# Gated mix of dilated attention and a 2-D Fourier filter: ScalarE's table read, one fp32 block, the gate sums and the issue order changed

## The chip, the cores and the metric

The kernel runs on one NeuronCore of a Trainium2 chip. A core has five engines with instruction streams of their own: TensorE (PE, the matmuls; its weight loads are listed as PEld), VectorE (DVE), ScalarE (ACT), GpSimd (POOL) and SyncE (SP, which here only starts transfers). Every engine takes its instructions strictly in the order in which the program issues them; engines wait for one another through semaphores. ACT, SP and POOL also start DMA transfers. The metric is the device time of one execution in microseconds (us).

## The reference, cut to what matters

Inputs are `x` (2048 x 640), the weights `wqkv` (640 x 1920) and `wo` (640 x 640), a filter `w_r`, `w_i` (2048 x 321) and the gate vector `gate_w` (640); all fp32.

```python
g = sigmoid((x * gate_w).sum(-1, keepdims=True))
# a: attention, 32 heads of 20, each row looks at rows s, s-2, ..., s-14
qkv = x @ wqkv
logits = einsum("bhsd,bhswd->bhsw", q, k gathered at s - 2*w) * 20**-0.5   # w = 0..7, masked below 0
a = (softmax(logits) weighted sum of v) @ wo
# b: filter in the frequency domain over both axes
b = irfft2(rfft2(x) * (w_r + 1j * w_i))
out = g * a + (1 - g) * b
```

## The kernel before

**Tiling.** Row `s = 16 p + j` of `x` lies on partition `p`, index `j`, so a step of two rows is a step of two in `j`. The even `j` ("par 0", tile `xe`) and the odd `j` ("par 1", tile `xo`) never meet in the attention. The columns of `wqkv` are cut into four groups `hg` of 8 heads. A unit `u = 4*par + hg` is one of the eight matmul stages `qkv0` to `qkv7`; it feeds two attention halves `a` and `b`.

**Precision.** A matmul in plain fp32 stands in the trace as two instructions and is slow, so nearly every fp32 product is split: `hi` is the operand rounded to fp32r (a cast on ACT), `lo` the remainder (a subtraction on DVE or POOL), and three fast products `hi*hi + hi*lo + lo*hi` take the place of one. `w` (weights) and `xe`, `xo` are such pairs. Only the blocks listed in `WHOLE` (line 1142) are multiplied in plain fp32, straight from the raw tiles `st`: before, these are row blocks 0 and 1 of the first 128 inner columns, the very first products of the kernel (`qkv_first`, line 679).

**Stages, in the order in which they were recorded.** `warm` (line 611): a DVE memset and six dummy matmuls. `load_first` (654): the five slices of the first column group, `in_w0`, started by ACT, and the five slices of the even rows, `in_xE`, started by SP (slice 0 in two pieces of 3 and 4 row blocks), then the casts on ACT and the subtractions on DVE. Then, for all eight units: products into one of seven PSUM banks, a copy to `ev` on ACT (two such tiles take turns, `store`, 722) and a DMA to DRAM (`qkvd`). The next weights go through `raw` (SP), a cast on ACT and a subtraction (`load_w`, 633). `attend` (746) reads `kt`, `q`, `vt` back: DVE and POOL form products `pr` and `pv` and DVE sums them to `L` and `o`; `o` goes to DRAM (`od`). On DVE and POOL `fold` (827) prepares the Fourier input, `cols` (855) and sixteen `freq` groups (877) transform it. Within a `freq` group PE forms `v` and `u`, ACT copies `vs`, DVE forms `ab`, PE forms `x` and `z`, ACT scales them into `X`, a pair of DMAs exchanges halves (`P<-X`), POOL and DVE multiply by the filter `wp` to `s`, and PE forms `g`, which ACT copies back into `zg`. `spatial` (1003) is the way back along the columns; `project_even` and `project_odd` (1085, 1101) multiply the attention output by `wo`. Odd projections need the attention of par 1, of which units 5 and then 4 come last.

**Gates.** `gates` (738) runs once, when all 16 row sums `z` are there: one exponential on ACT and four small DVE operations on 128 x 16 elements.

**What sets the order of the work.** The operations are first only recorded (`Plan.record`, 230): 3,656 of them, 1,977 on PE, 522 on DVE, 656 on ACT, 309 on POOL and 192 on SP. Then a list scheduler in the kernel file (`cost`, `order`, `forward`, `backward`, lines 249 to 437) gives each operation a made-up duration and latency (for instance 3.2 us for a transfer to land, 2 us added from POOL to ACT), computes due times and issues the operations in the order of the starts that it computes; a list of 32 random seeds (`FOUND`) perturbs it. That order is what the engines execute.

Of the kernel before, what the change touches and what calls it, by code (L numbers as in the profile page):

```python
# [11 lines left out]
ALU = mybir.AluOpType  # L12
# [16 lines left out]
PAGE = 512  # L29
# [120 lines left out]
class Op:  # L150
    __slots__ = ("i", "eng", "name", "call", "busy", "lat", "size", "preds", "succs", "chain", "tail", "start", "end", "early", "group", "of", "two")
# [12 lines left out]
class Plan:  # L164
# [4 lines left out]

    def __init__(self, nc):  # L170
        self.ops, self.places, self.past = [], {}, set()
        self.chain = self.group = ""
# [10 lines left out]
    def region(self, ap):  # L183
        off, pat = ap.offset, list(ap.ap)
        p0, p1 = 0, 1
        if ap.tensor.tag[:4] != "dram":
            p0 = off // pat[0][0]
            off, p1, pat = off - p0 * pat[0][0], p0 + pat[0][1], pat[1:]
        if ap.tensor.tag[:4] == "bank":
            off, pat = 0, [(1, 512)]  # L190
        idx = np.array([off])
        for st, n in pat:
            idx = (idx[:, None] + st * np.arange(n)).reshape(-1)
        return p0, p1, np.unique(idx)

    def touch(self, op, ap, write):

        if not hasattr(ap.tensor, "tag"):
            return
        tag, name = ap.tensor.tag, ap.tensor.name  # L200
        place = self.places.setdefault(tag, [name, {}, set()])
        if place[0] != name:
            assert name not in self.past, f"{name} used again after {place[0]}"
            self.past.add(place[0])
            self.places[tag] = place = [name, {}, {acc[0] for page in place[1].values() for acc in page}]
        pages, before = place[1:]
        if write:
            op.preds |= before
        p0, p1, idx = self.region(ap)
        size = PAGE if p1 > 1 else 1 << 30  # L210
        for pg in np.unique(idx // size):
            mine = idx[idx // size == pg]
            lo, hi, dense = mine[0], mine[-1], len(mine) == mine[-1] - mine[0] + 1
            kept = []
            for acc in pages.get(pg, ()):
                o, w, q0, q1, alo, ahi, adense, aidx = acc
                hit = o is not op and q0 < p1 and p0 < q1 and alo <= hi and lo <= ahi
                if hit and not (dense and adense):
                    hit = len(np.intersect1d(mine, aidx, assume_unique=True)) > 0
                if hit and (w or write):  # L220
                    op.preds.add(o)
                covered = write and hit and p0 <= q0 and q1 <= p1
                if covered:
                    covered = lo <= alo and ahi <= hi if dense else len(np.setdiff1d(aidx, mine, assume_unique=True)) == 0
                if not covered:
                    kept.append(acc)
            kept.append((op, write, p0, p1, lo, hi, dense, mine))
            pages[pg] = kept

    def record(self, eng, name, fn, a, k):  # L230
        op = Op()
        op.i, op.eng, op.name, op.chain, op.group = len(self.ops), eng, name, self.chain, self.group
        op.preds, op.succs, op.size, op.early, op.two = set(), [], 0, False, False
# [5 lines left out]
        aps = [v for v in list(a) + list(k.values()) if hasattr(v, "tensor") and hasattr(v, "ap")]  # L239
        out = k["out"] if "out" in k else a[0]  # L240
        ins = [v for v in aps if v is not out]
        for v in ins:
            self.touch(op, v, False)
        self.touch(op, out, True)
        op.of = out.tensor.name
        self.cost(op, out, ins, k)
        self.ops.append(op)

    def cost(self, op, out, ins, k):
        n = max(int(np.prod(v.shape[1:])) for v in [out] + ins[:1])  # L250
        if op.name == "dma_start":
            op.busy, op.lat = {"SP": 0.45, "ACT": 0.45, "POOL": 1.0}[op.eng], LAND
            op.size = int(np.prod(out.shape)) * 4
            op.early = not hasattr(ins[0].tensor, "tag")
        elif op.eng == "PE":
            n = int(np.prod(out.shape[1:]))
            if op.name == "transpose":
                op.busy = 0.109
            elif ins[-1].dtype == F32R:
                op.busy = n / 2400 + 0.018  # L260
            else:
                op.busy = 4 * n / 2400 + 0.006
            op.lat = 0.25
        elif op.eng == "DVE":
            op.busy, op.lat = 0.075 + n / 960, 0.12
            two = sum(v.tensor.tag[:4] not in ("bank", "qban") for v in ins) == 2
            if op.name == "scalar_tensor_tensor":
                op.busy += 0.06
            elif op.name == "reciprocal":
                op.busy += n * 0.007  # L270
            elif two:
                op.two = True
        elif op.eng == "ACT":
            strided = any(len(v.ap) > 2 and v.ap[-1][0] > 1 for v in [out] + ins)
            op.busy, op.lat = 0.12 + n * (1.75e-3 if strided else 0.78e-3), 0.15
            if len(ins) > 1:
                op.busy += 0.1
        else:
            spread = any(v.ap[-1][0] == 0 for v in ins)
            op.busy, op.lat = 0.09 + n * (2e-3 if spread else 2.25e-3), 0.14  # L280
        if op.eng in ("DVE", "ACT", "POOL") and not op.size:
            op.busy *= PACE

    def order(self):
        ops = self.ops
        for op in ops:
            op.lat += LATE.get(op.chain, 0.0) * (not op.size or op.chain in ("swap", "f"))
        for op in ops:
            for p in op.preds:
                p.succs.append(op)  # L290
        last = {}
        for op in reversed(ops):
            op.tail = max([s.tail + self.lag(op, s) for s in op.succs], default=0.0)
            if op.size:
                op.tail += op.size / RATE
            key = (op.eng, op.chain)
            if key in last and (op.eng == "PE" or op.chain and op.eng != "ACT"):
                op.tail = max(op.tail, last[key].tail)
            op.tail += op.busy
            last[key] = op  # L300
        span = max(op.tail for op in ops)
        for op in ops:
            op.early = max(0.0, span - op.tail - AHEAD) if op.early else 0.0
            op.tail += BIAS.get(op.chain, 0.0)
        best = self.turns(TURNS)

        kinds = [op.of for op in ops], [op.of.rstrip("0123456789_") for op in ops], [op.eng + op.of.rstrip("0123456789_") for op in ops]
        kinds = [[k[:4] if i else k for k in kind] for i, kind in enumerate(kinds)]
        self.kinds = []
        for kind in kinds:  # L310
            at = {k: i for i, k in enumerate(dict.fromkeys(kind))}
            self.kinds.append((len(at), np.array([at[k] for k in kind])))
        for seed in FOUND:
            for op, t in zip(ops, (best[1] + self.move(seed)).tolist()):
                op.tail = t
            best = self.turns(2)
        self.end = best[0]
        order = []
        for op, op.start, op.end in best[2]:
            order.append(op)  # L320
        return order

    def turns(self, n):

        runs = []
        for i in range(n + 1):
            tails = np.array([op.tail for op in self.ops])
            done = self.forward()
            end = max(op.end + op.lat for op in done)
            runs.append((end, tails, [(op, op.start, op.end) for op in done]))  # L330
# [880 lines left out]
```

## Time and profile before

| what | us |
|---|---|
| three runs | 460.13, 461.62, 462.81 |
| median | 461.62 |
| span of the profiled execution, first to last instruction | 459.8 |
| busy: PE, DVE, POOL, ACT | 442.6, 414.2, 364.3, 212.4 |

The profile is of one execution, on the one core. Its span leaves out what lies around the instructions; the median of the runs is 1.8 us longer. The busy time of PE counts a matmul that waits in the pipeline as busy. Times in the timeline count from the start of the span. `[idle before <-releaser]` behind a row says how long that engine was idle before it and whose end released it.

### The profile page before, as it was taken

How to read it: one execution, taken by the hardware profiler on the slowest of the kernel's cores; microseconds unless marked ns; L12 is line 12 of the kernel's file. 1: busy time of each engine (PE TensorE's matmuls, PEld its weight loads, DVE VectorE, ACT ScalarE, POOL GpSimd, SP SyncE). 2: the span in 40 equal slices, each digit the busy share in tenths (PEclk: the TensorE clock that was granted, in tenths of full speed). 3: DMA queues.
4: the chain of work that ended last, by engine and by line, in shares of the span. 5: the costliest groups of instructions: out<-in, count | busy, mean ns of one | idle time of the engine just before them, and what ended most of it. 6: DMA issues, size and time to landing. Idle time of an engine off the chain costs nothing.

```text
span 459.8 us, 7244 instructions
## 1 busy us (share of the span) xinstructions
PE 442.6 (96%) x2440; PEld 391.3 (85%) x2440; DVE 414.2 (90%) x522; ACT 212.4 (46%) x558; POOL 364.3 (79%) x316
## 2 busy tenths in 40 slices
PE   9999979999999999999997889999988999999996
PEld 6888868888889889899886778989977899988996
DVE  3898988999999998999999999899999998799574
ACT  4623235533326545246447666666554554342110
POOL 1158796699999988997997997886899997888820
PEclk9999989999999999999999999999999999999999
DMA  8998989768878979579979788889983331365842
GB/s 308 399 358 260 390 284 375 273 218 300 229 220 231 329 221 324 144 240 333 295 221 291 254 264 238 261 247 296 251 271 123 83 97 44 118 195 146 280 137 86
DMA packets 73956, 110.75 MB, mean 241 GB/s; under 512 B 21296, under 2 KB 50992, under 8 KB 73920
## 3 DMA queue, kind: packets, MB, share of 16 engines
q1 hardware_dynamic: 40192, 69.32, 46.6%
q10 hardware_dynamic: 32816, 36.97, 25.9%
q0 software_dynamic: 912, 4.00, 2.2%
q8 instruction: 19, 0.31, 0.3%
q14 instruction: 17, 0.14, 0.1%
HBM read 72.51 MB, written 32.84 MB: 229 GB/s over the span
## 4 chain that ended last, share of the span: by engine, by line
PE 78%; DMA 10%; POOL 4%; DVE 2%; ACT 2%; issue 1%; ACTq 1%; POOLq 0%; DVEq 0%
PE qkv L615 41%; PE woa L615 6%; PE wob L615 6%; DMA P<-X 5%; PE z L615 5%; PE oa L615 4%; PE ob L615 4%; DMA qkvd<-ev 3%; POOL P L615 3%; PE g L615 2%; DMA q0a<-qkvd 2%; PE hb L615 2%; PE ha L615 2%; PE v L615 2%; PE u L615 1%; PE oTp L615 1%
## 5 line engine op out<-in xcount | busy, mean ns | idle before, releaser
L615 PE MATMUL qkv<-w,xo 128*128 128x480 f32 (+1 forms) x480 | 110.8, 386 | 0.0
L615 PE MATMUL qkv<-w,xe 128*128 128x480 f32 (+1 forms) x474 | 106.2, 386 | 2.8 <-ACT w L615 2.8
L615 PEld LDWEIGHTS qkv<-w,xe 128*128 128x128 f32 x474 | 90.5, 191 | 18.7 <-ACT w L615 3.2
L615 PEld LDWEIGHTS qkv<-w,xo 128*128 128x128 f32 x480 | 89.8, 189 | 13.8 <-ACT zg L615 0.2
L615 ACT COPY ev<-qkv 128x480 f32<-128x480 f32 x64 | 35.1, 559 | 74.1 <-PE qkv L615 60.7
L615 PE MATMUL woa<-wo,oT 128*128 128x320 f32 x240 | 47.2, 318 | 0.6 <-DVE oT L615 0.3
L615 PE MATMUL wob<-wo,oT 128*128 128x320 f32 x240 | 46.9, 316 | 0.2 <-ACT ya L615 0.2
L615 POOL TENSOR_TENSOR P<-P,wp 128x963 f32<-128x963 f32 (+1 forms) x16 | 35.5, 2216 | 12.1 <-DMA P<-X 5.9
L615 PEld LDWEIGHTS woa<-wo,oT 128*128 128x128 f32 x240 | 37.7, 188 | 1.6 <-DVE oT L615 0.9
L615 PEld LDWEIGHTS wob<-wo,oT 128*128 128x128 f32 x240 | 37.8, 188 | 0.6 <-ACT ya L615 0.4
L615 POOL TENSOR_TENSOR fx<-fx 128x160 f32<-128x160 f32 (+1 forms) x16 | 12.2, 780 | 27.1 <-DVE fx L615 21.9
L615 POOL TENSOR_TENSOR w<-raw,w 128x480 fp32r<-128x480 f32 (+1 forms) x20 | 25.5, 1296 | 4.1 <-ACT w L615 4.1
L615 ACT CAST oT<-oTp 128x384 fp32r<-128x384 f32 (+1 forms) x32 | 13.4, 428 | 32.4 <-PE oTp L615 18.8
L615 PEld LDWEIGHTS g<-mm,s 128*128 128x128 f32 x150 | 21.2, 190 | 8.0 <-ACT zg L615 5.1
L615 PE MATMUL g<-mm,s 128*128 128x128 f32 x150 | 23.7, 280 | 4.1 <-ACT zg L615 3.2
L615 DVE TENSOR_TENSOR oT<-oTp,oT 128x384 fp32r<-128x384 f32 (+1 forms) x32 | 15.2, 484 | 10.0 <-ACT oT L615 9.9
L615 PE MATMUL oa<-gt,zg 128*128 128x161 f32 (+1 forms) x96 | 24.0, 344 | 0.0
L615 ACT CAST w<-raw 128x480 fp32r<-128x480 f32 (+1 forms) x30 | 17.2, 593 | 13.3 <-PE qkv L615 5.4
L615 PE MATMUL v<-bt,zc 128*128 128x240 f32 (+2 forms) x96 | 21.1, 325 | 1.9 <-ACT vs L615 1.8
L615 PE MATMUL ob<-gt,zg 128*128 128x161 f32 (+1 forms) x96 | 22.1, 344 | 0.0
L615 PE MATMUL u<-bt,zc 128*128 128x240 f32 (+2 forms) x96 | 20.3, 324 | 1.7 <-DVE ab L615 1.7
L615 PEld LDWEIGHTS u<-bt,zc 128*128 128x128 f32 x96 | 16.2, 189 | 4.1 <-DVE ab L615 1.2
(304 smaller groups left out, 1118.9 us busy)
## 6 DMA issues: line engine op xcount, KB each, us to landing
qkvd<-ev ACTq DMA_DIRECT2D x32, 480.0 KB, 4.8
wp<-in_ws SPq DMA_DIRECT2D x16, 642.0 KB, 5.6
raw<-in_wqkv SPq DMA_DIRECT2D x25, 240.0 KB, 6.8
fx<-in_x SPq DMA_DIRECT2D x8, 641.0 KB, 8.2
ot<-od SPq DMA_DIRECT2D x16, 320.0 KB, 3.4
P<-X ACTq DMA_DIRECT2D x30, 160.5 KB, 4.1
fd<-fx POOLq DMA_DIRECT2D x6, 640.0 KB, 7.5
f<-fd SPq DMA_DIRECT2D x6, 640.0 KB, 6.3
```

The source lines that it names most:

```text
L615: p.dve.memset(w, 0.0)
```

## The change

1. **Table read.** `warm` gets one more operation on ACT: a copy of one column of the zeroed tile. In the trace before, ACT's first computing instruction is preceded by an ACT_TABLE_LOAD.
2. **First transfers.** Slice 1 of `in_w0` is started by SP in place of ACT (`W0_SP`).
3. **One fp32 block for two.** `WHOLE` keeps (0, 0); block (1, 0) becomes three split products.
4. **Gate sums.** Three of the four DVE operations of `gates` (`1 + e`, `g - 1`, `1 - g`) become ACT operations; the reciprocal stays on DVE.
5. **Order.** The scheduler is gone. The operations are still recorded in the same sequence, and are issued in an order stored as a compressed string.

```diff
     def order(self):
-        ops = self.ops
...
-        return order
+        low, high = np.frombuffer(lzma.decompress(base64.b85decode("".join(ORDER.split()))), np.uint8).reshape(2, -1)
+        left, at = list(self.ops), low + 256 * high.astype(int)
+        assert len(at) == len(left)
+        return [left.pop(i) for i in at]
...
+ORDER = """
+T>t<81poj4|NsC0{{R326$?I)!2u1*Nf}?AmSE|uhAe8`yGLM)dM(g$Y~TpLBZIqd7Xw}I)19wZeN}MiGV`E!kd>$bRcBSWDq9b1%rA=d_}B$A_%Oua6Qw8m;-l*ba;C<oxwBJ%2Z0mn
...
         p.dve.memset(w, 0.0)
+        p.act.copy(self.one("tab", 1, tag="sign"), w[:, 0:1])
...
-            p.act.dma_start(self.wraw[0, t], self.ins["w0"][t])
+            (p.sp if t in W0_SP else p.act).dma_start(self.wraw[0, t], self.ins["w0"][t])
...
         p.act.activation(out=self.g, in_=self.z, func=AF.Exp, scale=-1.0)
-        p.dve.tensor_scalar_add(self.g, self.g, 1.0)
+        p.act.activation(out=self.g, in_=self.g, func=AF.Copy, bias=1.0)
         p.dve.reciprocal(self.g, self.g)
-        p.dve.tensor_scalar_sub(self.nng, self.g, 1.0)
-        p.dve.tensor_scalar(out=self.ng, in0=self.g, scalar1=-1.0, scalar2=1.0, op0=ALU.mult, op1=ALU.add)
+        p.act.activation(out=self.nng, in_=self.g, func=AF.Copy, bias=-1.0)
+        p.act.activation(out=self.ng, in_=self.g, func=AF.Copy, scale=-1.0, bias=1.0)
...
-WHOLE = ((0, 0), (1, 0))
+WHOLE = ((0, 0),)
+W0_SP = (1,)
```

The string unpacks to 3,659 numbers, two bytes each: 3,656 operations, one copy and two matmuls more. Each number is the place, in the list of recorded operations not yet issued, of the next one. Read out against the recorded sequence, the first operations of two queues are, side by side:

| ACT before | ACT after | SP before | SP after |
|---|---|---|---|
| start w0 slice 0 | start w0 slice 0 | start xE slice 0, blocks 0-2 | start xE slice 0, blocks 3-6 |
| start w0 slice 1 | start w0 slice 2 | start xE slice 0, blocks 3-6 | start w0 slice 1 |
| start w0 slice 2 | start w0 slice 3 | start xE slice 1 | start xE slice 1 |
| start w0 slice 4 | copy tab | start xE slice 2 | start xE slice 0, blocks 0-2 |
| start w0 slice 3 | start w0 slice 4 | start xE slice 3 | start row block 14 (xT) |
| cast w0 slice 0 | cast xE slice 0, blocks 3-6 | start xE slice 4 | start xE slice 3 |
| cast xE slice 0, blocks 0-2 | cast w0 slice 0 | start fx0 | start xE slice 2 |

Behind the six dummy matmuls, PE's list before begins with the two fp32 blocks; after, with seventeen split products of row blocks 3 to 6, and the one fp32 block left is the 24th entry of PE's list.

Four places further on, as entries of each engine's own list counted from 0:

| place | before | after |
|---|---|---|
| ACT: cast of `w2_3` | 71 | 65 |
| ACT: first copy of `ev1_4` / of `ev1_6` | 59 / 70 | 69 / 74 |
| PE: first product that reads `w2_3` / `w2_4` | 258 / 272 | 268 / 293 |
| PE: first product that reads `w3_3` / `w3_4` | 371 / 374 | 326 / 329 |

(`w2_3` is slice 3 of the weights of unit 2.)

More of the change, by code (lines that the diff above doesn't have):

```diff
@@ L1 @@
+import base64
+import lzma
 import sys
-from heapq import heapify, heappop, heappush
 import numpy as np
@@ L150 @@
 class Op:
-    __slots__ = ("i", "eng", "name", "call", "busy", "lat", "size", "preds", "succs", "chain", "tail", "start", "end", "early", "group", "of", "two")
+    __slots__ = ("i", "eng", "name", "call")
 class Engine:
@@ L170, in __init__ @@
     def __init__(self, nc):
-        self.ops, self.places, self.past = [], {}, set()
-        self.chain = self.group = ""
+        self.ops = []
         self.code = {}
@@ L196, in touch @@
[L196 to L228, printed above, removed]
@@ L230, in record @@
     def record(self, eng, name, fn, a, k):
         op = Op()
-        op.i, op.eng, op.name, op.chain, op.group = len(self.ops), eng, name, self.chain, self.group
-        op.preds, op.succs, op.size, op.early, op.two = set(), [], 0, False, False
+        op.i, op.eng, op.name = len(self.ops), eng, name
         line = sys._getframe(2).f_lineno
@@ L238, in record @@
         op.call = (code, {"fn": fn, "a": a, "k": k})
[L239 to L246, printed above, removed]
-        self.ops.append(op)
[L249 to L282, printed above, removed]
@@ L284, in order @@
-    def order(self):
-        ops = self.ops
[L286 to L320, printed above, removed]
-        return order
@@ L323, in turns @@
[L323 to L330, printed above, removed]
-            if i < n:
-                self.backward(end)
-        return min(runs, key=lambda r: r[0])
-    def move(self, seed):
-        rng = np.random.default_rng(seed)
-        n, kind = self.kinds[rng.integers(3)]
-        shift = rng.choice([0.6, 2.0, 6.0, 15.0]) * rng.normal(size=n)
-        return (shift * (rng.random(n) < rng.choice([0.03, 0.1, 0.4, 1.0])))[kind]
@@ L465, in staged @@
+HnU*@@RtAPIC%5
+"""
 def staged(gens, n):
```

170 lines of the change are left out of this document (31 added, 139 removed).

## The prediction

> **What bounds the kernel now.** The busy times on the page come first, then the waits of PE over the whole span, then the table of stretches.
>
> ```profile
> PE 442.6 (96%) x2440; PEld 391.3 (85%) x2440; DVE 414.2 (90%) x522; ACT 212.4 (46%) x558; POOL 364.3 (79%) x316
> ```
> ```profile
> PE g L615 <- ACT zg L615: 3.2, 5, 1.3
> PE qkv L615 <- ACT w L615: 2.8, 1, 2.8
> PE v L615 <- ACT vs L615: 1.8, 1, 1.8
> PE u L615 <- DVE ab L615: 1.7, 2, 1.0
> ```
> ```profile
> 4.00:16.00 12.00, 12.00 (x44) 8.77 (x45) 7.54 (x14) 8.92 (x17) 0.00 (x0) 1.00 1.04 390
> ...
> 145.00:235.00 90.00, 90.00 (x477) 79.53 (x476) 86.42 (x76) 41.23 (x111) 81.79 (x63) 1.00 0.87 272
> 235.00:305.00 70.00, 63.79 (x375) 55.35 (x374) 65.05 (x101) 45.58 (x131) 58.97 (x50) 1.00 0.85 255
> 305.00:353.00 48.00, 45.05 (x288) 40.15 (x288) 45.59 (x68) 27.69 (x75) 41.34 (x31) 1.00 0.84 250
> 353.00:420.00 67.00, 66.43 (x415) 60.08 (x414) 60.36 (x86) 31.52 (x81) 58.68 (x49) 1.00 0.36 107
> 420.00:460.00 40.00, 36.18 (x255) 35.83 (x253) 26.16 (x58) 4.91 (x12) 17.43 (x22) 1.00 0.49 162
> ```
>
> In the table the columns are the stretch, its length, busy time (count) of PE, PEld, DVE, ACT and POOL, granted PE clock, DMA share and GB/s. PE is the bound, with 17.2 us of the 459.8 idle; DVE is close behind: 86.42 of 90 us in the longest stretch. So a gain has two forms: an idle place of PE that closes, or work that leaves DVE. The idle of PE sits in one hole near 62 us, and in the Fourier groups between 235 and 353 us (70.00 - 63.79 = 6.2 us and 48.00 - 45.05 = 2.9 us). Elsewhere PE is dense, so no stage can give more than these holes.
>
> **The hole at 62 us.** The timeline shows what ACT did while PE waited, and the stretches beside it show the clock.
>
> ```profile
> 63.85 0.56 ACT L615 COPY ev<-qkv 128x480 f32<-128x480 f32 x1 [2.24 <-DMA qkvd<-ev]
> 64.31 0.60 ACT L615 CAST w<-raw 128x480 fp32r<-128x480 f32 x1
> ...
> 64.95 10.37 PE L615 MATMUL qkv<-w,xe 128*128 128x480 f32 x39 [2.79 <-ACT w L615]
> ```
> ```profile
> 61.60:65.00 3.40, 0.61 (x4) 0.20 (x2) 3.37 (x3) 1.16 (x4) 3.40 (x4) 1.00 0.57 167
> 65.00:68.40 3.40, 3.40 (x9) 2.84 (x10) 2.17 (x2) 1.65 (x6) 3.40 (x5) 0.51 0.86 251
> 68.40:71.80 3.40, 3.40 (x17) 2.93 (x16) 3.33 (x4) 1.77 (x5) 1.98 (x2) 0.99 1.04 376
> ```
>
> ACT takes its list in order. The copy of `ev1_6` stood ahead of the cast of `w2_3` and waited for an `ev` transfer to free its tile; the cast needed no such thing, and PE needed the cast. The hole is 2.8 us, and behind it PE ran 3.4 us at a clock of 0.51: 9 matmuls where the next stretch has 17, so 8 x 0.2 = 1.6 us more (0.2 us is 3.40 / 17). **Price: 4.4 us.**
>
> By the stored order the cast of `w2_3` is ACT's 65th entry and the first copies of `ev1_4` and `ev1_6` are the 69th and 74th, so it no longer stands behind that wait. PE reads `w2_4` first at its entry 293, not 272: 21 matmuls later. What can come instead is late `w3`: PE now asks for `w3_4` 45 matmuls sooner, at entry 329. The pace for this is in the row below, 38.33 / 175 = 0.219 us.
>
> ```profile
> 23.83 38.33 PE L615 MATMUL qkv<-w,xe 128*128 128x482 f32 x175
> ...
> 74.75 0.59 ACT L615 CAST w<-raw 128x480 fp32r<-128x480 f32 x1
> ```
>
> Counting from the hole (entry 258, at 62.0 us), entry 329 falls at 62.0 + 71 x 0.219 = 77.5 us; the cast of `w3_4` ended at 75.3 us before, and its transfer and cast stand at nearly the same places of their lists. The margin is 2 us. I take 4.0 of the 4.4 us as gained; bounds: 4.4, and -4.4 if the same hole opens twice.
>
> **The gate sums.** Here are the four operations of DVE, the exponential of the same shape on ACT, and what stood around the longest.
>
> ```profile
> L615 ACT ACTIVATE g<-z x1: 223/223/223, 249.1 to 249.1; 128x16 f32<-128x16 f32 x1
> L615 DVE TENSOR_SCALAR g<-g x1: 823/823/823, 249.7 to 249.7; 128x16 f32<-128x16 f32 x1
> L615 DVE RECIPROCAL g<-g x1: 253/253/253, 250.5 to 250.5; 128x16 f32<-128x16 f32 x1
> L615 DVE TENSOR_SCALAR ng<-g x1: 4199/4199/4199, 270.5 to 270.5; 128x16 f32<-128x16 f32 x1
> L615 DVE TENSOR_SCALAR nng<-g x1: 518/518/518, 384.2 to 384.2; 128x16 f32<-128x16 f32 x1
> ```
> ```profile
> 269.85 2.66 POOL L615 TENSOR_TENSOR pv7b<-vt7b,L7b 128x640 f32<-128x640 f32 x2
> ...
> 270.45 4.20 DVE L615 TENSOR_SCALAR ng<-g 128x16 f32<-128x16 f32 x1
> ...
> 271.11 3.54 DVE L615 TENSOR_REDUCE L6b<-pr6b 128x64 f32<-128x1280 f32 x1
> ...
> 272.40 2.23 POOL L615 TENSOR_TENSOR P<-P,wp 128x963 f32<-128x963 f32 x1
> ...
> 274.73 0.94 PE L615 MATMUL u<-bt,zc 128*128 128x240 f32 x4 [0.97 <-DVE ab L615]
> ```
>
> Sixteen columns need 0.25 us on DVE, yet one of these took 4.20 us. It ended at 274.65, within 0.1 us of the end of the POOL work beside it (272.40 + 2.23 = 274.63), and the reduction issued behind it ended at 274.65 as well (271.11 + 3.54): DVE stood still until POOL was done, and PE then waited 0.97 us for `ab`. Gone from DVE are 0.82 + 4.20 + 0.52 = 5.5 us. ACT gets three operations of 0.22 us, and it is busy 45.58 of 70 us there; queued behind them are copies such as `vs`, which then come up to 0.7 us later. How much of the 5.5 us reaches the end isn't in a row: at least nothing, at most all of it less 0.7. DVE is over 90% busy up to 420 us, but PE would have to use the time. I take half, **2.5 us**; bounds 0 and 4.8.
>
> A rule stands against this edit: the Trainium skill, "ScalarE: Activation LUTs", section "Rules for kernel authors", sends plain additions and multiplications to VectorE and not ScalarE. Here 0.22 us on ACT stands against 0.52 to 4.20 us on DVE, so the trace disagrees.
>
> **The start.** These are the rows of the first microseconds.
>
> ```profile
> 0.74 3.51 ACTq L615 DMA_DIRECT2D st<-in_w  x5
> 0.75 5.48 SPq L615 DMA_DIRECT2D st<-in_xE  x6
> ...
> 1.06 2.93 PE L615 MATMUL warmed<-warm 128*128 128x128 f32 x12 [1.06 <-DVE warm L615]
> ...
> 3.94 3.41 PE L615 MATMUL qkv<-st,st 128*128 128x482 f32 x4
> 4.28 1.28 ACT L615 ACT_TABLE_LOAD   x1 [4.28 <-DMA st<-in_w]
> ...
> 5.58 0.59 ACT L615 CAST w<-st 128x482 fp32r<-128x482 f32 x1
> ...
> 6.07 0.51 ACT L615 CAST xe<-st 128x384 fp32r<-128x384 f32 x1
> ...
> 6.63 17.58 PE L615 MATMUL qkv<-w,xe 128*128 128x482 f32 x76
> ```
>
> The table read takes 1.28 us ahead of the first cast. After three transfers are issued (0.74 + 3 x 0.70 = 2.85 us; 0.70 is 3.51 / 5) the new copy lets it run until 4.1 us, and the copy itself ends by 4.3 us. The fourth issue stands behind the copy, so slice 4 may start 0.7 us later than before; it is cast last. On SP the moved transfer delays every later issue by 5.48 / 6 = 0.9 us, but the DMA share is 1.04 between 4 and 16 us, so the data, not the issues, set the landings. ACT can thus cast 1.3 us earlier. PE loses its fill, though: the two fp32 blocks ran from 3.94 to 6.63 us while ACT was still at it, and now PE's first product needs two casts, which end at about 4.3 + 0.6 + 0.6 = 5.5 us. Two blocks stand for six split products; between 5.5 and 6.63 us PE can do at most five at the pace of 17.58 / 76 = 0.23 us, and three at the half clock. So PE is 0.3 to 0.8 us behind. The block itself gives a little back: two of the four passes (half of 2.7 us, or half of that at full clock) go and 3 x 0.23 = 0.69 us come, a gain of 0 to 0.65 us. Together **+0.3 us**; bounds -0.4 and +2.4, the latter with a late clock, below.
>
> **The order elsewhere.** The stored order moves most operations; the rows can't price that. The waits of the Fourier groups (9.1 us of PE idle) are short chains PE, ACT, DVE, POOL and a transfer; in the stored order PE has more work between `u`, `v` and `x` in groups 1 to 3 (about 4.1, 3.3 and 2.7 us for 3.1, 1.3 and 1.2), less between `z` and `g` in group 4 (8.9 for 11.9); these are estimates, matmul counts of the two orders times the median distance of starts of each shape in the trace. I take **-1.0 us**; bounds -6 (two thirds of the waits) and +4 (half as much again). At the end, from 420 us, 36.18 of 40 us are PE work that stays: nothing.
>
> **Sum:** -4.0 - 2.5 + 0.3 - 1.0 = -7.2 us; 459.8 - 7.2 = 452.6 us of span. With the 1.8 us by which the median stands above this span: **454.4 us**, 1.6% less.
>
> **The rivals.**
> *DVE sets the pace.* PE comes out of the first stages 4 us sooner and waits for DVE at 235 us instead. For it: DVE is busy 96% from 145 to 235 us. Against it: 5.5 us leave DVE. Then only 1.5 us remain: 460.1 us (458 to 463).
> *The gate time stays on DVE.* The instruction next in line meets the same POOL work and waits as long. For it: the reduction behind was held too. Against it: the reciprocal of the same 16 columns took 0.25 us, so not every DVE operation waits in this way. Then the 2.5 us go: 456.9 us. The skill's rule above would lead to this time too.
> *Late clock.* PE now idles from about 4.0 to 5.5 us, right behind the dummies (1.06 + 2.93); if the full clock comes one 3.4 us stretch later, that costs the 1.6 us of the row 65.00:68.40: 456.0 us. Before, the idle hole at 62 us was followed by just that stretch. The Trainium skill, "TensorE: Matmul & The Clock Gate", section "Part 1: The HAM clock gate", says that the clock is judged in free-running windows of 3.4 us; the half-clock stretch here, 3.4 us, agrees.
> *Slower: `w3` late.* Place: 77 us, the casts of `w3_3` and `w3_4`, whose transfers are not moved forward while PE's demand is. If they end over 2 us later than before (transfers of `kt` and `raw` share the queue), PE stands again, and once more with the third column group mixed into units 2 and 7; each hole costs 4.4 us with its clock. With both, and a late clock: 454.4 + 8.8 + 1.6 = 464.8 us.
> *The order is much better.* All of the hole, 4.8 us from DVE and 5 us of the Fourier waits: 14 us, 447.5 us.
> *It does not do what it says:* the table read stays behind the first landing. Then 1.3 us are lost at the start: 455.7 us.
>
> **Chances.** Forecast 0.36; gates nothing 0.08; late clock 0.08; much better 0.15; DVE paces 0.18; `w3` late 0.12; table read unmoved 0.03. Half a per cent, 2.3 us, is about what a measurement of this kernel can tell from no change, so faster is below 459.3 and slower above 463.9. Faster: all cases below 457 and a quarter of "DVE paces", 0.74; same: the rest of that, 0.14; slower 0.12. The range leaves out most of "`w3` late" and the lower part of "much better": 446 to 463 us.
>
> **What would show it.** Right: an ACT_TABLE_LOAD before 4.2 us; no PE wait on `w` near 62 us and a clock of 1.00 from 65 to 68 us; three ACT rows of 0.2 us for the gates and no DVE row over 3 us near 270; under 7 us of PE idle in the Fourier groups in place of 9.1. Wrong: a PE wait on `w` between 75 and 80 us, a larger DVE idle, or the same waits in the Fourier groups with other names.

## The result, and the profile after

The changed kernel took 472.94 us (median of 4 runs, 470.31 to 477.00) beside 460.88 us for the kernel before (4 runs, 457.98 to 462.81): a ratio of 1.029 [1.021, 1.037]. It is slower, and the time lies 10 us above the range of the prediction. The profiled execution took 473.41 us, with a span of 471.4 us. Runs of one kernel spread over several us (those of the kernel before, over all chips of this study, from 455.9 to 466.3 us), so ratios to the kernel before on the same chip are used below.

The page of the changed kernel, with busy times, the chain that ended last, and two groups (busy, mean, then idle before and its releaser):

```profile
PE 451.7 (96%) x2441; PEld 392.9 (83%) x2441; DVE 411.6 (87%) x519; ACT 213.9 (45%) x562; POOL 363.3 (77%) x316
...
PE 74%; DMA 15%; DVE 4%; ACT 3%; POOL 2%; ACTq 1%; issue 1%; POOLq 0%; DVEq 0%
...
L387 PE MATMUL qkv<-w,xo 128*128 128x480 f32 (+1 forms) x480 | 117.3, 391 | 4.4 <-ACT ev L387 2.5
L387 PE MATMUL qkv<-w,xe 128*128 128x480 f32 (+1 forms) x477 | 110.4, 391 | 1.1 <-ACT w L387 1.1
```

DVE did less work than before (411.6 for 414.2 us) in a longer span: its idle time grew from 45.6 to 59.8 us, 14 us. The wait for `w` of 2.8 us is gone from the even rows' products; the odd rows' products, which waited for nothing before, now wait 4.4 us. The stretches, in the columns of the table in the prediction:

```profile
65.00:145.00 80.00, 76.97 (x352) 64.71 (x350) 74.35 (x63) 30.41 (x80) 69.56 (x58) 0.98 0.76 237
145.00:235.00 90.00, 87.49 (x463) 75.52 (x462) 85.30 (x75) 42.74 (x114) 78.61 (x62) 1.00 0.86 279
235.00:305.00 70.00, 65.47 (x340) 54.02 (x340) 62.22 (x92) 41.90 (x128) 58.78 (x49) 0.95 0.82 249
305.00:353.00 48.00, 47.05 (x301) 42.04 (x300) 44.91 (x68) 30.04 (x81) 38.25 (x28) 1.00 0.85 258
```

PE worked through the whole of 145 to 235 us before (90.00 of 90 us, 477 matmuls); now it idles there for 2.5 us, and for 3.0 us between 65 and 145 us. These are the stretches that the prediction called dense. The stretches of the Fourier groups idle a little less (4.5 + 1.0 us between 235 and 353 us, 9.1 before), but part of 235 to 305 us runs at the half clock (mean 0.95). The first product of `v` starts 6.0 us later than before (240.09 for 234.08 us), so about half of the 11.6 us by which this execution is longer comes ahead of the Fourier groups, and half behind their start.

Three steps can be read directly. First the stretches around the old hole:

```profile
61.60:65.00 3.40, 3.40 (x17) 2.94 (x17) 2.85 (x3) 2.94 (x8) 3.34 (x3) 1.00 0.75 180
65.00:68.40 3.40, 3.40 (x17) 2.92 (x16) 3.37 (x4) 1.76 (x5) 3.00 (x6) 1.00 1.05 321
```

The hole at 62 us and its half-clock stretch are gone, as predicted: 17 matmuls for 4, and 17 for 9. Next the gate rows, by shape (columns: count, busy, mean ns):

```profile
L387 ACT ACTIVATE nng<-g 128x16 f32<-128x16 f32 x1 | 0.2, 214 | 0.0
L387 ACT ACTIVATE g<-g 128x16 f32<-128x16 f32 x1 | 0.2, 210 | 0.0
L387 ACT ACTIVATE ng<-g 128x16 f32<-128x16 f32 x1 | 0.2, 210 | 0.0
```

Three operations of 0.21 us stand in place of 0.82, 4.20 and 0.52 us on DVE. Last the start, in the timeline and in stretches:

```profile
2.16 1.28 ACT L387 ACT_TABLE_LOAD   x1 [2.16 <-issue]
...
3.92 0.62 ACT L387 CAST xe<-st 128x512 fp32r<-128x512 f32 x1 [0.28 <-DMA st<-in_xE]
...
5.09 1.98 PE L387 MATMUL qkv<-w,xe 128*128 128x482 f32 x4 [1.10 <-ACT w L387]
```
```profile
3.60:7.00 3.40, 2.30 (x7) 1.73 (x7) 2.42 (x4) 2.25 (x5) 0.00 (x0) 1.00 1.02 379
7.00:10.40 3.40, 3.40 (x11) 2.80 (x10) 2.08 (x4) 2.73 (x6) 0.00 (x0) 1.00 1.05 414
10.40:13.80 3.40, 3.40 (x16) 2.62 (x15) 3.40 (x7) 3.29 (x7) 0.00 (x0) 1.00 1.04 409
```

The table was read 2.1 us earlier, and PE's first product came at 5.09 us, not 3.94. The clock column says 1.00 here, but 11 matmuls in 7.00 to 10.40 us beside 16 in the next stretch show the slower pace: the full clock came one stretch late, which was a rival. So the table read, the gate rows and the hole at 62 us came out as forecast, and the start with one of its rivals. What these rows leave as the likely place of the loss is the order, and that was tested.

### The profile page after: what moved, and what is told of

Read it like the earlier page. It is cut to its first block, busy times and chain, and to the rows that moved or that the text cites. A ratio compares the mean times of both kernels' runs of the same rounds, so it can differ in the third digit from the quotient of the medians.

```text
span 471.4 us, 7247 instructions
## 1 busy us (share of the span) xinstructions
PE 451.7 (96%) x2441; PEld 392.9 (83%) x2441; DVE 411.6 (87%) x519; ACT 213.9 (45%) x562; POOL 363.3 (77%) x316
## 4 chain that ended last, share of the span: by engine, by line
PE 74%; DMA 15%; DVE 4%; ACT 3%; POOL 2%; ACTq 1%; issue 1%; POOLq 0%; DVEq 0%
PE qkv L387 35%; PE woa L387 7%; PE wob L387 7%; DMA qkvd<-ev 5%; PE z L387 5%; PE ob L387 3%; PE oa L387 3%; DMA P<-X 3%; PE v L387 3%; PE g L387 2%; PE u L387 2%; DMA q5b<-qkvd 2%; PE hb L387 2%; PE ha L387 2%; PE oTp L387 2%; POOL P L387 2%
## 5 line engine op out<-in xcount | busy, mean ns | idle before, releaser
L387 PE MATMUL qkv<-w,xo 128*128 128x480 f32 (+1 forms) x480 | 117.3, 391 | 4.4 <-ACT ev L387 2.5
L387 PE MATMUL qkv<-w,xe 128*128 128x480 f32 (+1 forms) x477 | 110.4, 391 | 1.1 <-ACT w L387 1.1
L387 PEld LDWEIGHTS qkv<-w,xo 128*128 128x128 f32 x480 | 87.6, 189 | 19.7 <-ACT zg L387 4.1
L387 PE MATMUL wob<-wo,oT 128*128 128x320 f32 x240 | 42.3, 318 | 0.0
L387 PE MATMUL woa<-wo,oT 128*128 128x320 f32 x240 | 42.0, 317 | 0.3 <-ACT oT L387 0.3
L387 PEld LDWEIGHTS wob<-wo,oT 128*128 128x128 f32 x240 | 36.0, 188 | 1.3 <-ACT ya L387 0.5
L387 POOL TENSOR_TENSOR fx<-fx 128x158 f32<-128x158 f32 (+1 forms) x16 | 11.7, 751 | 24.5 <-DVE fx L387 24.5
L387 PE MATMUL oa<-gt,zg 128*128 128x161 f32 (+1 forms) x96 | 21.8, 344 | 0.0
L387 PEld LDWEIGHTS v<-bt,zc 128*128 128x128 f32 x96 | 15.4, 192 | 4.3 <-ACT vs L387 2.8
L387 ACT COPY zg<-g 128x384 f32<-128x384 f32 (+1 forms) x32 | 13.6, 425 | 11.1 <-PE g L387 4.6
```

Of the source, the lines that this page charges most:

```text
L387: p.dve.memset(w, 0.0)
```

## The experiments

Each kernel below computes the whole reference. `issued` is the list that the string unpacks to; `old` is the order of the scheduler, `stored` that of the change.

**The change in halves.** `edits_old_order` has the four edits in the old order; `stored_order_alone` undoes the edits; `stored_front` takes the stored order for the 1,671 operations that the old order issues ahead of the first Fourier group, `stored_back` for those behind it. The three new lines below are those of `edits_old_order`, `stored_front` and `stored_back`.

```diff
-issued = stored
+issued = old
+issued = [k for k in stored if k in ahead] + [k for k in old if k not in ahead]
+issued = [k for k in old if k in ahead] + [k for k in stored if k not in ahead]
```

> The four edits (table read early, slice 1 of w0 on SP, one fp32 block, gate sums on ACT) in the order of the kernel before. Theory A, the stored order costs the time: this is 1 to 4 us faster than before, 457 to 460 us, with no DVE row of 4 us for the gates and the hole at 62 us still there. Theory B, one of the edits costs it (the start at half clock, or ACT held up by the gates): 466 to 473 us.

> The stored order with all four edits undone (two fp32 blocks, no early copy, all of w0 on ACT, gates on DVE). Theory A: 472 to 477 us, as slow as the changed kernel or some us more, since the edits help. Theory B: 459 to 463 us, as the kernel before.

> All edits; the operations that the old order issues before the first Fourier group stand in the stored order, those behind it in the old order. Theory A with the loss in the matmul stages: 6 to 8 us slower than before, 466 to 469 us, the first product of v near 240 us as in the changed kernel (234 us before). Theory A with the loss in the Fourier groups: within 2 us of before.

> All edits; the old order up to the first Fourier group, the stored order behind it. Theory A with the loss in the Fourier groups: 5 to 7 us slower than before, 465 to 468 us. With the loss in the matmul stages only: 457 to 460 us. If both halves lose alone what they lose together, the two runs add up to the 12 us.

| kernel | us, median | ratio to the kernel before |
|---|---|---|
| edits, old order | 462.82 | 1.007 [1.004, 1.011] |
| stored order alone | 474.79 | 1.034 [1.028, 1.040] |
| stored in front | 470.88 | 1.026 [1.019, 1.033] |
| stored behind | 466.01 | 1.014 [1.007, 1.021] |

The stored order alone carries all of the loss, and most of it lies ahead of the Fourier groups. (`stored_front` and `stored_back` both contain the edits, 1.007 by themselves.)

**The edits one by one**, in the old order: `gates_alone` has the gate sums on ACT, `start_alone` the table read, slice 1 on SP and the one fp32 block.

> The old order; of the four edits only the gate sums on ACT. If the 4 us that DVE stood behind POOL reach the end: 2 to 4 us faster than before (0.5 to 0.9%). If DVE's time is not what sets the end there, or the next DVE operation takes over the wait: within 1 us of before. If the three ACT operations hold up PE: 1 us or more slower.

> The old order with the early table read, slice 1 of w0 on SP and one fp32 block for two, and the gates on DVE. If the start is what the edits lose (PE without its fill, a late or a broken clock): 3 to 5 us slower than before, and with gates_alone it adds up to edits_old_order. If the start is neutral: within 1 us of before.

`gates_alone` gave 0.999 [0.995, 1.003], so the gates are worth at most 2.3 us (0.005 x 460). DVE's busy time fell by 3.0 us (414.2 to 411.2) and not by 5.5: the row of 4.20 us overlaps the rows behind it, which end with it or just after. Nor is that row a fixed cost. `start_alone` has the gates on DVE, in the old order, with the same POOL operations beside them, and there it took 0.95 us:

```profile
L384 DVE TENSOR_SCALAR ng<-g x1: 946/946/946, 270.9 to 270.9; 128x16 f32<-128x16 f32 x1
```

It ended there at 271.9 us, with the first of the POOL operations beside it (`pv7b`, to 271.83 us), and not also with the next one. `start_alone` gave 1.008 [1.004, 1.013], 1.6 to 5.9 us. Its stretches show a part of what the start costs:

```profile
4.25:7.66 3.41, 1.43 (x4) 0.46 (x3) 1.36 (x3) 1.48 (x4) 0.00 (x0) 1.00 1.04 385
7.66:11.07 3.41, 3.10 (x8) 2.61 (x9) 3.33 (x7) 3.03 (x7) 0.00 (x0) 0.50 1.03 417
```

With only one fp32 block PE ran out of work (1.43 of 3.41 us), and the stretch behind ran at a clock of 0.50. The granted clock over whole executions fits this: its median over the runs was 0.989 in `start_alone` and 0.995 in the kernel before on the same chip, and 0.989 and 0.999 for `edits_old_order`. As an estimate, 0.006 and 0.010 of 460 us are 3 and 5 us. Not all of it lies at the start: the profile of `start_alone` has two more half-clock stretches, from 247 and 257 us, and that of `edits_old_order`, with the same start, has none there and one from 245 us. Why stretches so far behind the start come with it was not found.

**Theories on the front that did not explain the loss.** In the stored order the 15 products of a `qkv` block are spread, on average, over 66 entries of PE's list, 29 in the old; a PSUM bank is held that much longer, and some `ev` tiles stand half full (`ev3_0` for 25.5 us, where it was 1 to 13 us before). `stored_closed` moves the products of each block of units 1 to 7 together (28 entries). `stored_held_ev` gives the four tiles that stand longest a place of their own. `stored_old_start` has the first 127 operations as before, without the edits of the start.

```diff
+        self.evh = ring("ya")
...
-            self.ev = self.evr.next(f"ev{u}_{jj}", 6, 2, HC)
+            self.ev = (self.evh if (u, jj) in HELD else self.evr).next(f"ev{u}_{jj}", 6, 2, HC)
...
+HELD = ((1, 0), (2, 2), (3, 0), (7, 2))
```

> The changed kernel, but on PE the fifteen products of a matmul block of units 1 to 7 are moved together towards the block's last one (a block then spans 28 matmuls of PE's list in place of 66; 29 in the old order). All else keeps the stored order. Theory C, the stored order loses in the matmul stages because it holds the seven PSUM banks open: 5 to 8 us faster than the changed kernel, 464 to 468 us. Rival, it loses there because copies and transfers stand in another order on ACT and SP: within 2 us of the changed kernel, 470 to 475 us.

> The changed kernel with a tile of their own for the four ev pairs that it keeps half filled longest (ev1_0, ev2_2, ev3_0, ev7_2: 13 to 26 us from the first copy to the transfer, against 1 to 13 us before); the load of wor0, which has that tile next, is issued behind them. Theory D, the stored order loses in the matmul stages because half-filled ev tiles leave one tile for all other copies, so banks stay full and PE stops: the hole at 109 us with its half clock goes, 3 to 5 us faster than the changed kernel, 468 to 470 us. Rival: the holes come from late transfers whatever the tiles, within 2 us of the changed kernel.

> The first 127 operations (up to the first copy of ev) in the old order and without the early copy, the moved slice and the split block; gates on ACT; everything behind in the stored order. If the new start (PE waits for two casts where the fp32 blocks ran, full clock at 10.2 us for 7.05) costs what the first 20 us show: 3 us faster than the changed kernel, 469 to 471 us. If a later start is absorbed by later waits: within 1 us of it.

Measured: `stored_closed` 502.58 us, 1.101 [1.094, 1.108], 30 us worse than the changed kernel, which neither theory had expected; `stored_held_ev` 1.026 [1.020, 1.032]; `stored_old_start` 1.022 [1.017, 1.027], lower by about what the start costs (0.007), though the intervals overlap. The waits of PE, of `stored_closed` and then of `stored_held_ev`:

```profile
PE z L381 <- ACT ev L381: 11.2, 6, 7.4
PE qkv L381 <- ACT ev L381: 5.4, 5, 2.8
```
```profile
PE qkv L386 <- ACT ev L386: 3.3, 3, 2.7
PE z L386 <- ACT ev L386: 2.6, 2, 2.3
```

The holes keep their name, ACT's copy to `ev`, and change their place. Neither closing the blocks nor freeing the held tiles took the loss away. That closed blocks ask ACT for copies in bursts may be why `stored_closed` is so slow; that was not tested.

**Where the loss lies.** These kernels cut between the stored and the old order at four matmuls of the old order; `ahead` is what the old order issues ahead of the 259th, 451st, 542nd or 641st, at about 62, 107, 127 and 145 us. `stored_swap` is the changed kernel with the exchange transfers `P<-X` started by SP.

```diff
-issued = stored
+ahead = set(old[:old.index(matmuls[258])])
+issued = [k for k in stored if k in ahead] + [k for k in old if k not in ahead]
```

> All four edits; the stored order for the 484 operations that the old order issues ahead of the 259th matmul (about 62 us), the old order behind them. It stands between the edits in the old order (1.0074) and the stored order up to the Fourier groups (1.026). If the loss of the front arises at the start and in the first units (theory 'early'), this is at 1.02 or above, about 470 us by a before of 460. If it arises behind 62 us (theory 'later': the holes at 109, 147, 180 and 220 us), this is at 1.007 to 1.010, about 463 to 465 us. If it is spread evenly over the first 235 us, 1.012.

> As stored_to_64, but with the stored order for the 1,145 operations ahead of the 641st matmul (about 145 us). If the loss lies between 62 and 145 us (the hole at 109 us and its half clock stand there), this is at 1.022 to 1.026 while stored_to_64 is near 1.01. If it lies in the stages behind 145 us (units 6 and 7 mixed with the preparation of the Fourier input), it is near 1.01 as well. If it is spread evenly, 1.019.

> The changed kernel with one edit: the exchange transfers of X are started by SP in place of ACT. In the old order the same edit took 4.4 us away. If what the stored order loses behind 235 us is ACT standing at these issues, this is 4 us or more below 472.9 in the runs of the changed kernel, a ratio of 1.02 or less to the kernel before. If the stored order's holes there come from the order of its matmuls, it stays at 1.026 to 1.03.

> As stored_to_64, with the stored order for the 824 operations ahead of the 451st matmul of the old order (about 107 us), the old order behind them. stored_to_64 gave 0.996 and stored_to_145 1.018. If the loss comes from the order between 62 and 107 us (units 2 and 3), this is at 1.012 or above; if it comes with the first products of the odd rows behind 107 us, where the changed kernel has its hole at 109 us, it is at 0.996 to 1.000.

> As stored_to_105, cut at the 542nd matmul (about 127 us), so that the first blocks of unit 7 come in the stored order but not the units' mixing with the Fourier input behind them. If the hole at 109 us with what follows from it carries the loss, this is at 1.008 to 1.015; if the mixing of z with the odd units behind 127 us carries it, 0.996 to 1.002.

| stored order up to | ratio to the kernel before |
|---|---|
| nothing (edits, old order) | 1.007 [1.004, 1.011] |
| 62 us | 0.996 [0.993, 0.999] |
| 107 us | 1.020 [1.015, 1.025] |
| 127 us | 1.018 [1.014, 1.022] |
| 145 us | 1.018 [1.013, 1.024] |
| Fourier groups (235 us) | 1.026 [1.019, 1.033] |
| all | 1.029 [1.021, 1.037] |

Up to 62 us the stored order gains 1.1%; between 62 and 107 us, the units 2 and 3, it loses 2.4% (1.020 / 0.996), 11 us. What comes behind adds at most 1%, within the intervals. The gain goes with the granted clock, as far as its medians tell: the median is 0.010 below that of the kernel before in `edits_old_order` and equal to it in `stored_to_64` (0.996). The loss does not: 0.995 for 0.996 in `stored_to_105`. `stored_swap` gave 1.034 [1.027, 1.040]: the exchange issues are not what is lost behind 235 us.

The two neighbours, `stored_to_64` and `stored_to_105`, differ only in where 340 operations stand. Some of these stand ahead of 62 us in the stored order: a hole of 1.98 us that `stored_to_64` has at 32 us is not there in `stored_to_105`. First two stretches of the one, then of the other:

```profile
65.00:145.00 80.00, 80.00 (x383) 69.27 (x382) 76.35 (x65) 35.18 (x92) 70.71 (x58) 1.00 0.81 265
145.00:235.00 90.00, 90.00 (x478) 79.56 (x477) 88.85 (x78) 42.11 (x114) 83.78 (x66) 1.00 0.88 278
```
```profile
65.00:145.00 80.00, 76.64 (x362) 65.69 (x361) 68.63 (x59) 30.25 (x79) 61.99 (x52) 1.00 0.76 239
145.00:235.00 90.00, 86.17 (x450) 75.99 (x449) 87.51 (x77) 43.04 (x114) 83.07 (x66) 0.96 0.86 268
```

DVE does 7.7 us less in the first stretch (68.63 for 76.35) and cannot make it up in the next, where it is busy 87.51 of 90 us. The span is 7.6 us longer (465.3 for 457.7). That the two numbers agree is chance, since DVE had done 2.6 us more by 65 us; what ties them is followed below. ACT's timeline shows what DVE waited for; `stored_to_64` first:

```profile
92.52 1.02 ACT L384 COPY ev<-qkv 128x480 f32<-128x480 f32 x2 [0.20 <-ACT qbank L384]
...
100.15 0.37 ACTq L384 DMA_DIRECT2D q2a<-qkvd  x1
...
108.75 0.30 ACT L384 COPY qbank<-q2a 128x160 f32<-128x160 f32 x1 [4.00 <-DVE pr1b L384]
```

Then `stored_to_105`, ACT and, in a second fence, DVE:

```profile
85.57 1.35 ACT L385 CAST xo<-xt 128x640 fp32r<-128x640 f32 x2 [4.42 <-DMA fd<-fx]
...
89.79 0.56 ACT L385 COPY ev<-qkv 128x480 f32<-128x480 f32 x1 [2.34 <-DMA qkvd<-ev]
...
106.30 2.04 ACTq L385 DMA_DIRECT2D q2a<-qkvd  x1
113.47 0.30 ACT L385 COPY qbank<-q2a 128x160 f32<-128x160 f32 x1 [8.20 <-DMA q2a<-qkvd]
...
115.56 0.55 ACT L385 COPY ev<-qkv 128x480 f32<-128x480 f32 x1
```
```profile
113.81 1.49 DVE L385 TENSOR_TENSOR pr1b<-kt1b,qbank 128x1280 f32<-128x1280 f32 x1 [5.16 <-ACT qbank L385]
```

In the stored order the casts of `xo` and a copy to `ev` stand ahead of other work and wait 4.42 and 2.34 us for transfers. The last store of unit 2 is started at 98.69 us (93.58 in `stored_to_64`), and the load of `q2a`, which the stored order puts further back in ACT's list, at 106.30 and not 100.15 us. The copy that needs it stands there 8.20 us; it is the very next entry of ACT's list, where five others stand between the two in `stored_to_64` and four in the changed kernel, so the length of this wait is in part made by the cut. The `qbank` copies that DVE needs and the `ev` copy that PE needs, both in ACT's list behind it, wait with it: 5.16 us of idle time on DVE, and 2.07 us on PE, for `ev`, at 116 us. From there the delay can be followed to PE:

```profile
142.40 4.62 PE L385 MATMUL z<-fc,fx 128*128 128x128 f32 x40
...
147.78 0.30 ACT L385 COPY qbank<-q3a 128x160 f32<-128x160 f32 x1 [4.13 <-DVE pr2b L385]
...
150.21 0.58 ACT L385 COPY zg<-z 128x512 f32<-128x512 f32 x1 [0.44 <-ACT ev L385]
...
150.85 29.01 PE L385 MATMUL qkv<-w,xo 128*128 128x480 f32 x120 [3.83 <-ACT zg L385]
```

At 142.40 us PE is only 1.0 us behind `stored_to_64` (141.44), but DVE is 6 us behind (it reduces `m1b` at 127.41 and not 121.46 us). ACT's `qbank` copy waits for DVE, the copies to `zg` stand behind it in ACT's list, and PE waits 3.83 us for them and runs at half the clock from 149.6 to 156.5 us. At the next `z` block PE is 7.6 us behind (179.69 for 172.10), and it stays so to the end.

The changed kernel has waits of ACT of the same kind, with another instruction at the head:

```profile
84.51 1.35 ACT L387 CAST xo<-xt 128x640 fp32r<-128x640 f32 x2 [3.17 <-DMA fd<-fx]
...
88.58 0.56 ACT L387 COPY ev<-qkv 128x480 f32<-128x480 f32 x1 [2.19 <-DMA qkvd<-ev]
...
105.10 0.89 ACTq L387 DMA_DIRECT2D q2a<-qkvd  x1
...
111.50 0.56 ACT L387 COPY ev<-qkv 128x480 f32<-128x480 f32 x1 [5.26 <-DMA qkvd<-ev]
...
113.89 0.62 ACT L387 COPY qbank<-q2a 128x160 f32<-128x160 f32 x2 [1.42 <-DMA q2a<-qkvd]
```
```profile
112.11 1.99 PE L387 MATMUL qkv<-w,xo 128*128 128x480 f32 x5 [2.49 <-ACT ev L387]
```

Here the way to the loss is another: DVE waits only 0.70 us for `qbank`, and PE itself stands 2.49 us for the late `ev` copy, with a half-clock stretch behind it.

The changed kernel and the cuts at 107, 127 and 145 us have these waits of ACT for a transfer, of over 2 us, at 85 and 89 us, and one or more between 109 and 141 us (`stored_front` some 4 us later); the kernel before has none between 64 and 161 us, `stored_to_64` none between 62 and 161. One such wait alone does not cost the time: `start_alone` and `gates_ev_table_swap`, in the old order, have one of 3.42 and 3.69 us at 78 us, for `q1a`. The transfers themselves are slow in this place too. The issues between 96 and 112 us, with the KB of each and the time to landing, in the changed kernel and in `stored_to_64`:

```profile
qkvd<-ev ACTq DMA_DIRECT2D x2, 480.0 KB, 5.2
...
q2a<-qkvd ACTq DMA_DIRECT2D x1, 320.0 KB, 8.8
```
```profile
qkvd<-ev ACTq DMA_DIRECT2D x2, 480.0 KB, 3.3
...
q2a<-qkvd ACTq DMA_DIRECT2D x1, 320.0 KB, 5.8
```

Whether the loads of `raw` that SP starts nearby hold them up wasn't tried, and no run moved these entries of ACT's list alone. So the cuts show that the order of the units 2 and 3 carries the loss; the way by which it does so is read from the traces.

**A better kernel.** In the old order: `gates_third_ev` gives units 0 to 3 a third `ev` tile and has the gates on ACT; `gates_ev_table` adds the early table read alone; `gates_ev_table_swap` also lets SP start the exchange. `stored_64_ev_swap` is `stored_to_64` with the tile and the swap.

```diff
+        self.evr3 = ring("ya", "ev0", "ev1")
...
-            self.ev = self.evr.next(f"ev{u}_{jj}", 6, 2, HC)
+            self.ev = (self.evr3 if u < 4 else self.evr).next(f"ev{u}_{jj}", 6, 2, HC)
...
-            A.dma_start(P[0:64, 1:3], X[64:128])
-            A.dma_start(P[64:128, 1:3], X[0:64])
+            S.dma_start(P[0:64, 1:3], X[64:128])
+            S.dma_start(P[64:128, 1:3], X[0:64])
```

> The old order, gate sums on ACT, and for units 0 to 3 a third tile for ev, so that a copy waits for the transfer of three pairs ago and not two. If the hole at 62 us is that wait: it is gone in every profile, and the run is 2 to 4 us faster than gates_alone. If the cast of w2_3 is late for another reason (its own transfer): as gates_alone.

> The old order with gate sums on ACT, the third ev tile and the early table read alone (both fp32 blocks and all of w0 on ACT as before). If the early table read is good once PE keeps its fp32 blocks: 0.5 to 1.5 us faster than gates_third_ev, 454 to 456 us where before has 458 to 461. If the start of PE is set by the landings: as gates_third_ev.

> As gates_ev_table, with the exchange transfers P<-X started by SP in place of ACT. If the hole of 2.3 to 2.9 us near 243 us, which every run of the old order has, comes from ACT standing in the issue of these transfers (2.15 us for two at 245.74 us before): the hole goes, 2 to 4 us faster than gates_ev_table. If SP then stands instead and holds up the loads behind: the same or slower.

> stored_to_64 with a third store tile for the units 0 to 3 and with the exchange transfers of X started by SP. The best kernel so far has these two in the old order with the gates and the table read (0.986, 453.9 us). If the stored order's gain in the first 62 us (stored_to_64 stands 1.1 per cent under the edits in the old order) adds to theirs, this is at 0.980 or below, about 451 us; the hole at 31 us that waits for a copy to ev goes. If the third tile had taken the same hole at 62 us already, it is at 0.986 again.

| kernel | us, median | ratio to the kernel before |
|---|---|---|
| third ev tile, gates | 457.36 | 0.997 [0.993, 1.002] |
| and table read | 458.26 | 0.995 [0.992, 0.998] |
| and swap | 453.88 | 0.986 [0.982, 0.990] |
| stored to 62 us, tile, swap | 453.61 | 0.988 [0.984, 0.992] |

The swap did most of it; the two steps ahead of it in the table lie within the intervals. Around it in the kernel before, then in `gates_ev_table_swap`:

```profile
245.74 2.15 ACTq L615 DMA_DIRECT2D P<-X  x2
247.99 0.43 ACT L615 COPY vs<-v 128x321 f32<-128x321 f32 x1 [2.27 <-DVE L6a L615]
```
```profile
241.21 0.53 ACT L385 ACTIVATE X<-z,sign 128x321 f32<-128x321 f32 x1
241.80 0.43 ACT L385 COPY vs<-v 128x321 f32<-128x321 f32 x1
```

ACT spent 2.15 us starting two transfers, with `vs`, which PE waits for, behind them; with SP starting them `vs` follows at once. (The first row names DVE's `L6a` as the releaser; in the second kernel `L6a` ends at 243.8 us, behind the copy, so the copy does not need it.) In the stored order the same swap gained nothing (1.034 for 1.029). The stored order's gain up to 62 us does not add to this, against what was expected. The third tile removes the wait for `ev` at 62 us, but the cast of `w3_2`, which stands just ahead in ACT's list, then waits 3.57 to 3.78 us for its own load, and PE still waited for `w`: 0.41 us in `gates_third_ev`, 1.92 us in `gates_ev_table`. Whether the tile and the stored order up to 62 us take the same time out was not settled.

## Why the prediction was wrong, by its own steps

**The hole at 62 us (-4.0).** Right in mechanism: it is gone, and `w3` was not late. The size rests on one execution: the same copy ahead of the same cast made PE wait 1.42 us in `gates_alone`, with no half clock, and not at all in `edits_old_order` and `start_alone`. The stored order up to 62 us gained 1.1%, 5 us, but only in ratios that include everything else it moves there.

**The gates (-2.5).** The durations on ACT were right to 0.02 us. The term was mis-sized: 0.999 [0.995, 1.003] leaves at most 2.3 us of gain, and none fits as well. The 5.5 us added up rows that overlap (DVE's busy time fell by 3.0 us), and took a wait of one execution, 4.20 us, for the rule; it was 0.95 us in `start_alone`. The rival that the next instruction would wait as long did not come: the reduction took 1.48 us in `gates_alone`. The rule of the Trainium skill that the prediction weighed ("ScalarE: Activation LUTs", "Rules for kernel authors") would have left these on VectorE; the traces disagree by the rows, 0.21 us on ACT beside 0.49 to 4.20 us on DVE for the three operations moved, but the whole time does not tell the two apart.

**The start (+0.3, up to +2.4).** Mis-sized: 1.008 is 3.8 us [1.6, 5.9]. The first product came at 5.09 us, forecast 5.5; the late clock, kept out of the sum as a rival with a chance of 0.08, came in the changed kernel, and in `start_alone` a half-clock stretch 3.4 us behind the first full clock. But that is 1.6 us, and the profile of `edits_old_order` shows neither; by the clocks of the runs the rest of the 3.8 us is half-clock time further behind, which no step of the prediction had. With the gates at nothing, the start makes up the 1.007 of `edits_old_order`.

**The order elsewhere (-1.0, bounds -6 and +4).** This step failed. It priced the order only in the Fourier groups, where PE had idle time, after the sentence "Elsewhere PE is dense, so no stage can give more than these holes". That is true of a gain, and says nothing of a loss: a dense stage has the most to lose. The runs showed a loss between 62 and 107 us, 11 us by the ratios and 7.6 us by the two profiles, where the prediction had no term. The figures that would have warned were quoted in it: DVE at 86.42 of 90 us, so that a delay of DVE ahead of 145 us can hardly be made up before the Fourier groups, and ACT, whose list had just been seen to stand behind one late store for 2.2 us.

**The rivals.** "`w3` late" was of the right kind, an ACT list standing behind transfers that the order had moved, at the wrong place (77 us, the weights) and with the wrong transfers (`fd`, the `ev` stores and `q2a`). "DVE sets the pace" was read as a limit to the gain; in `stored_to_105` a late DVE passed the loss on, through ACT, to PE, while in the changed kernel PE waits for ACT directly. The tail (0) is right within 2 us: from the start of the last copy of `g` to `zg` to the end 104.8 us (471.4 - 366.6) for 106.8 (459.8 - 353.0).

What stays open: whether moving those entries of ACT's list alone would take the loss away, why the transfers between 96 and 112 us land late, and how the last 1% behind 145 us arises; there the intervals overlap. In the profiled execution 5.6 us come behind the start of the Fourier groups, and two half-clock stretches there make 3.4 of them.

## What to carry to other kernels

When an order is replaced, price the stages without idle time first, for what they can lose: look for the engine with a strict list that feeds two others (here ACT, 45% busy), and ask of each of its entries which transfer it waits for and what stands behind it. Cutting between the old and the new order at four places found the stage, where three kernels built on theories about single waits had not. A price read from one profile should be looked for in a second one: the hole and the gate wait, 4.0 and 2.5 us of the forecast, were smaller or absent in some other kernels with the same order in that place. And where an engine both computes and starts transfers, moving the starts to SP was worth more in the old order (0.995 to 0.986) than all of the change's edits.

## What the runs showed of the hardware

The clock falls in stretches of 3.41 us, or two of them together (149.6 to 156.5 us in `stored_to_105`). In the changed kernel the granted clock is halved from 112.59 to 116.00 us, behind the hole at 109 us, and again from 266.19 and from 279.84 us, each time for 3.41 us; one of them in two stretches of the table:

```profile
112.00:115.40 3.40, 3.29 (x9) 2.79 (x10) 2.67 (x4) 1.06 (x5) 3.40 (x3) 0.59 0.63 169
115.40:118.80 3.40, 3.40 (x15) 2.78 (x15) 3.37 (x3) 1.12 (x3) 1.01 (x2) 0.91 0.20 75
```

Holes of about the same size did not always bring it: in `stored_to_145` PE waited 2.10 us at the same place (111.82 us) and the clock stayed full for the whole run, in the changed kernel it waited 2.49 us and the clock was halved. The Trainium skill, "TensorE: Matmul & The Clock Gate", section "Part 1: The HAM clock gate", says that the activity windows run freely and do not start with the kernel; the traces agree: with the same start, the full clock came at 7.05 us in the kernel before, at 5.95 us in `gates_alone` and at 5.09 us in `gates_third_ev`. A hole here cost its length, or its length and 1.6 us, or more, and single profiles of kernels of this spread should not be compared to less than that.

The first copy behind the early table read followed it at once (1.28 us from 2.16 us, the copy at 3.45 us), so the early read cost no more than its own 1.28 us.
